# A windowed-attention and sticky-router kernel: the TensorE work of each attention step put in the order of its tile shapes, and two PSUM rings exchanged

## The chip, the core and the metric

The kernel runs on one core of a Trainium2 chip. The metric is the device time of one execution in microseconds (us). The kernel before was timed in three runs; their median is 696.66 us. The engines are TensorE (PE in the profile, with its weight loads as PEld), VectorE (DVE), ScalarE (ACT), GpSimd (POOL) and SyncE (SP), which issues most transfers. The program keeps eight PSUM tiles of 128 x 512 fp32 values, ps0 to ps7, one bank each; TensorE writes its results there, and VectorE and ScalarE read them.

## The reference, cut to what matters

Eight batches of eight heads are attended to. Each head has 512 local tokens, which see the local tokens at most 32 positions away and all 32 global tokens, and 32 global tokens that see all. The 576 rows of 512 values that come out per batch go through a router (eight experts, with a gate that may keep the expert of the row before) and then through the chosen expert, two layers of 512 x 1024.

```python
s_ll = np.where(abs(pos_q - pos_k) <= 32, scale * q_l @ k_l.T, -1e9)
a_l = softmax(concat([scale * q_l @ k_g.T, s_ll]))        # local rows
out_l = a_l @ concat([v_g, v_l])
out_g = softmax(scale * q_g @ concat([k_g, k_l]).T) @ concat([v_g, v_l])
x = concat([out_g, out_l])                                # 576 x 512 per batch
logits = x @ w_gate; local_gate = sigmoid(x @ w_local)
e = argmax(logits) if s == 0 or local_gate < 0.5 else the expert of the row before
out = softmax(logits)[e] * (relu(x @ w1[e]) @ w2[e])
```

## The kernel before, in words

The program has an attention part, the first 240 us or so, a routing part that is worked in between, and the experts' products, which fill the rest. The change is in the attention part alone (class Attn).

**Units and steps.** The work of a batch is cut into six units: four local ones, l0 to l3, each a pair of heads, and two global ones, g0 and g1, each two pairs. They run in the order l0, l1, g0, l2, g1, l3 (the list `order` in `run`), 48 units in all. One pass of the loop in `run` is called a step here. A step computes the scores of one unit (`nx`) and finishes the unit of two steps earlier (`st`). The six steps of a batch are numbered by the unit whose scores they compute:

| step | scores of | finishes |
|---|---|---|
| 0 | l0 | g1 of the batch before |
| 1 | l1 | l3 of the batch before |
| 2 | g0 | l0 |
| 3 | l2 | l1 |
| 4 | g1 | g0 |
| 5 | l3 | l2 |

**What a step issues.** The instructions of each engine stand in the order in which the code records them (the schedule is manual). For a local unit, in two halves hb of 256 rows each:

- `l_s` (L238, L243): a product with an identity puts the mask into a PSUM bank (L238, a tile of 128 x 128), and eight products per half add the scores (L243, stationary tiles of 128 rows by 64 columns). The two products of a pair fill different column halves.
- `l_max` (L248, L250, on VectorE): the row maximum, and the scores minus the maximum, written to SBUF. This frees the bank. `l_exp` (L254) is the exponential on ScalarE.
- `l_t` (L260, L262): two steps later, eight 128 x 128 transposes, and two copies on ScalarE out of PSUM.
- `l_av` (L276): the products with v, stationary tiles of 128 rows by 32 columns, 16 per half, into one bank; then on VectorE the row sums plus 1e-9 (L279), their reciprocals (L281), and the scaled output into the tile xa (L284). L284 frees the bank.

A global unit does the same with `g_s` (L296, 64 columns), `g_max` (L304, L306), `g_exp`, `g_t` (L328, six transposes) and `g_av` (L339, 32 columns).

**The router's pieces.** When a unit of a batch is finished, a piece of x = xa is transposed: `f1` (L352, four transposes of 128 x 128, one for each local unit, copied by ScalarE at L353) and `f1g` (L359, one transpose for the global rows). After the fourth come the router products `f2` (L367) and `f2g` (L375), with 32 columns, then `f3`: four transposes of the logits (L385), a small product (L388), and three VectorE instructions (L390 to L392). They stand in one list, `fin`, from which `fpiece` takes one piece at two places of a step: behind the first scores of the step, and ahead of the v products of the second half.

**Routing in between.** `drip` (called in `l_max`, `g_max`, `l_av`, `g_av`) records one of the routing's small VectorE instructions at a time (`keys`, `probs`, from batch 4 on also `stage_a`, the ranking of tokens by expert).

**PSUM.** The eight banks make three rings, taken in turn: `ps_s`, ps0 to ps3, for scores (and for f3's transposes); `ps_t`, ps4 and ps5, for the transposes l_t, g_t, f1 and f1g; `ps_o`, ps6 and ps7, for l_av, g_av, f2, f2g and f3's small product. Whoever takes a bank waits until its last user has been read out.

A word on tile shapes: 128, 64 and 32 below are the columns of the stationary tile, as the profile's rows have them (128*128, 128*64, 128*32).

## Time and profile before

| what | value |
|---|---|
| median of the three runs (lowest, highest) | 696.66 us (694.63, 696.86) |
| the profiled execution | 694.06 us |
| its span, first to last instruction | 692.3 us |
| PE busy / PEld / DVE / ACT / POOL, share of the span | 97% / 81% / 62% / 50% / 30% |
| DMA | 151.44 MB, mean 219 GB/s |
| TensorE clock granted over the span | 0.995 |

The span is the time from the first to the last instruction of the profiled execution; 1.8 us of its time lie around it. Busy shares are of the whole span. The rows of a timeline give a start, a length from the first start to the last end, the engine, the line and operation, the output and the inputs, the tile (rows*columns of the stationary operand), the number of records, and in brackets the idle time before. A matmul's end is modelled, and matmuls overlap in the rows, so lengths of PE rows overlap too: what a row costs is read here from its start to the start of the next row. An fp32 product appears as two records. A few matmul records are missing.

### The profile page before, as it was taken

How to read it: one execution, taken by the hardware profiler on the slowest of the kernel's cores; microseconds unless marked ns; L12 is line 12 of the kernel's file. 1: busy time of each engine (PE TensorE's matmuls, PEld its weight loads, DVE VectorE, ACT ScalarE, POOL GpSimd, SP SyncE). 2: the span in 40 equal slices, each digit the busy share in tenths (PEclk: the TensorE clock that was granted, in tenths of full speed). 3: DMA queues.
4: the chain of work that ended last, by engine and by line, in shares of the span. 5: the costliest groups of instructions: out<-in, count | busy, mean ns of one | idle time of the engine just before them, and what ended most of it. 6: DMA issues, size and time to landing. Idle time of an engine off the chain costs nothing.

```text
span 692.3 us, 18408 instructions
## 1 busy us (share of the span) xinstructions
PE 670.5 (97%) x7253; PEld 561.1 (81%) x7253; DVE 426.2 (62%) x1050; ACT 342.9 (50%) x614; POOL 207.7 (30%) x342
## 2 busy tenths in 40 slices
PE   9999999999989899998998999999999999999995
PEld 7777777777767787897887988889898889888994
DVE  7878677688887777995517535335354516255572
ACT  4555556555455674653326625344444325255553
POOL 7634334343674301033013303040404020133023
PEclk9999999999999999999999999999999999999999
DMA  8956957866856497777418647337475417265673
GB/s 318 405 220 233 346 193 309 310 248 231 299 196 273 147 356 243 260 243 245 174 60 308 232 149 239 102 117 235 145 225 191 140 61 231 66 222 193 212 270 103
DMA packets 43011, 151.44 MB, mean 219 GB/s; under 512 B 7965, under 2 KB 9245, under 8 KB 38688
## 3 DMA queue, kind: packets, MB, share of 16 engines
q1 hardware_dynamic: 35536, 126.92, 51.6%
q0 software_dynamic: 6960, 21.90, 9.5%
q8 instruction: 77, 1.26, 0.7%
q14 instruction: 150, 1.23, 0.6%
q10 hardware_dynamic: 288, 0.13, 0.1%
HBM read 130.55 MB, written 19.69 MB: 217 GB/s over the span
## 4 chain that ended last, share of the span: by engine, by line
PE 60%; DVE 3%; issue 1%; ACT 0%; POOL 0%; POOLq 0%; DVEq 0%; ACTq 0%
PE ps L1267 29%; PE ps L1256 27%; PE ps L1210 3%; DVE wq L1165 1%; DVE wp L1165 1%; PE ps L1004 0%; PE ps L1379 0%; DVE xl L1165 0%; DVE xT L994 0%; POOL xa L1196 0%; DVE xT L996 0%; POOLq L1427 0%; DVE wp L1213 0%; PE ps L276 0%; DVE wq L1371 0%
## 5 line engine op out<-in xcount | busy, mean ns | idle before, releaser
L1273 POOL DMA_INDIRECT out_dram<-y,tk x39 | 40.4, 1036 | 317.6 <-ACT y L1272 246.3
L1267 PE MATMUL ps<-wp,wq 128*128 128x512 f32 x504 | 128.4, 402 | 1.0 <-ACT wq L1370 1.0
L1267 PEld LDWEIGHTS ps<-wp,wq 128*128 128x128 f32 x504 | 93.5, 190 | 21.1 <-ACT wq L1370 1.2
L1256 PE MATMUL ps<-wp,wp 128*128 128x256 f32 (+5 forms) x672 | 109.3, 322 | 0.2 <-issue 0.2
L1256 PEld LDWEIGHTS ps<-wp,wp 128*128 128x128 f32 x672 | 103.6, 188 | 5.3 <-issue 0.4
L1259 DVE SCALAR_TENSOR_TENSOR wq<-ps,wq 128x256 fp32r<-128x256 f32 (+5 forms) x80 | 41.7, 525 | 72.8 <-ACT wq L1258 62.6
L1213 DVE TENSOR_TENSOR wp<-ps,wp 128x512 fp32r<-128x512 f32 x40 | 27.5, 691 | 78.9 <-ACT wp L1212 78.8
L1258 ACT ACTIVATE wq<-ps 128x256 fp32r<-128x256 f32 (+5 forms) x80 | 37.3, 468 | 78.3 <-PE ps L1256 68.8
L191 POOL TENSOR_SCALAR_AFFINE_SELECT qbd<-raw 64x512 f32<-64x512 f32 x62 | 44.4, 716 | 103.3 <-PE ps L243 85.5
L243 PE MATMUL ps<-kx,qbd 128*64 128x128 f32 x1024 | 71.3, 280 | 0.2 <-issue 0.2
L1272 ACT ACTIVATE y<-ps,pp 128x512 f32<-128x512 f32 x39 | 26.9, 690 | 77.7 <-PE ps L1267 71.1
L243 PEld LDWEIGHTS ps<-kx,qbd 128*64 128x64 f32 x1024 | 55.1, 137 | 12.2 <-issue 7.8
L248 DVE TENSOR_REDUCE mx<-ps 128x4 f32<-128x512 f32 x64 | 43.9, 687 | 29.9 <-PE ps L243 29.9
L1165 DVE TENSOR_TENSOR wp<-raw,wp 128x1024 fp32r<-128x1024 f32 x47 | 57.0, 1217 | 2.8 <-ACT wp L1155 2.8
L254 ACT ACTIVATE pe<-pe 128x512 f32<-128x512 f32 x64 | 40.7, 637 | 31.7 <-DVE pe L250 31.7
L1196 POOL DMA_INDIRECT xa<-xs,idx x42 | 50.9, 1212 | 17.1 <-issue 9.4
L1155 ACT CAST wp<-raw 128x1024 fp32r<-128x1024 f32 x49 | 50.8, 1047 | 0.8 <-ACT hh L1258 0.5
L1212 ACT CAST wp<-ps 128x512 fp32r<-128x512 f32 x40 | 23.4, 590 | 53.9 <-PE ps L1210 53.3
L250 DVE TENSOR_TENSOR pe<-ps,mx 128x512 f32<-128x512 f32 x64 | 44.0, 688 | 1.6
L276 PEld LDWEIGHTS ps<-v,pt 128*32 128x32 f32 x2048 | 33.4, 110 | 13.1 <-issue 7.3
L276 PE MATMUL ps<-v,pt 128*32 128x65 f32 x2048 | 42.8, 222 | 1.1 <-issue 0.4
L262 ACT COPY pt<-ps 128x512 f32<-128x512 f32 x64 | 34.9, 610 | 17.6 <-PE ps L260 17.6
(280 smaller groups left out, 1183.3 us busy)
## 6 DMA issues: line engine op xcount, KB each, us to landing
raw<-in_w_dram SPq DMA_DIRECT2D x78, 512.0 KB, 4.1
v<-in_vw_dram SPq DMA_DIRECT2D x32, 1040.0 KB, 9.8
raw<-in_qk_dram SPq DMA_DIRECT2D x32, 528.0 KB, 8.2
xa<-in_w_dram SPq DMA_DIRECT2D x26, 512.0 KB, 5.2
xT<-in_w_dram SPq DMA_DIRECT2D x20, 512.0 KB, 3.5
xs<-xa SPq DMA_DIRECT2D x8, 1056.0 KB, 4.9
qgb<-in_qg_dram SPq DMA_DIRECT2D x8, 128.0 KB, 3.5
xa<-xs,idx POOLq DMA_INDIRECT x42
```

What stands on the lines that cost most here:

```text
L191: self.nc.gpsimd.affine_select(out=out, in_=in_, pattern=pat, compare_op=ALU.is_ge, fill=0.0, base=0, channel_multiplier=0)
L243: nc.tensor.matmul(sp[64 * t2:64 * t2 + 64, t], qbd[:, w], kf[:, f:f + P], start=False, stop=True, skip_group_check=True)
L248: nc.vector.tensor_reduce(out=mx, in_=st["sp"], axis=AX.X, op=ALU.max)
L250: nc.vector.tensor_tensor(out=st["pe"][:, 4 * hb:4 * hb + 4], in0=st["sp"], in1=mx.broadcast_to([P, 4, P]), op=ALU.subtract)
L254: self.nc.scalar.activation(out=pe, in_=pe, func=AF.Exp, scale=SCALE)
L276: nc.tensor.matmul(o[32 * w4:32 * w4 + 32, g, h], pt[:, 2 * g + w4 // 2, w4 % 2, h, :], v[:, w, h * (D + 1):(h + 1) * (D + 1)], start=True ...
L1155: nc.scalar.copy(out=hi, in_=raw)
L1165: (nc.gpsimd if pool else nc.vector).tensor_tensor(out=lo, in0=raw, in1=hi.bitcast(F32), op=ALU.subtract)
L1196: self.nc.gpsimd.indirect_dma_start(out=self.xr[j] if k == "early" else self.xr4[:, j], out_offset=None, in_=src, in_offset=bass.IndirectO ...
L1256: nc.tensor.matmul(ph, a[:, dc, fs], b_[:, dc, n0:n1], start=(n == 0), stop=(n == 11))
L1259: nc.vector.scalar_tensor_tensor(out=hl[:, fc, n0:n1], in0=ph, scalar=0.0, in1=hh[:, fc, n0:n1].bitcast(F32), op0=ALU.max, op1=ALU.subtract)
L1267: nc.tensor.matmul(py, a[:, fc, js], b_[:, fs], start=(fc == 0 and k == 0), stop=(fc == 7 and k == 2))
```

## The change

Within a step, the instructions of TensorE are put in the order of their tile shapes: first all that uses 128 columns (the transposes l_t or g_t, the masks of both halves, which a new function `l_m` issues ahead of the scores, and the pieces f1, f1g and the transposes of f3, now a function `f3t` of their own), then the scores of both halves (64 columns), then all that uses 32 columns (f2, f2g, f3's small product and the v products of both halves). The one list of pieces becomes two, `wide` for those of 128 columns and `thin` for those of 32, each piece with the step from which it may run; up to two of each are taken in a step. The pieces f1 of l0, l1 and l2 run two steps after their unit was finished, f1 of l3 one step after, f1g two steps after, f2 one and f3 two steps after l3 was finished. And f1 and f1g take their banks from `ps_o` (ps6, ps7) instead of `ps_t`, while f2, f2g and f3's small product take theirs from `ps_t` (ps4, ps5) instead of `ps_o`.

With the order on TensorE the order on VectorE changes too: L248 and L250 of both halves (L252 and L254 in the changed code) come ahead of the three instructions of each half's v products.

```diff
+    def l_m(self, st):
+        nc = self.nc
+        b, pr = st["u"]
+        if pr == 0:
+            self.cur[b]["xa"] = self.xa()
+            self.cur[b]["xg"] = self.xg()
+        st["pe"] = self.pe()
+        st["sps"] = [self.bank(self.ps_s) for _ in range(2)]
+        for hb, sp in enumerate(st["sps"]):
+            mo = sp.rearrange("p t (k c) -> p t k c", c=32)[:, :, 0::3, :]
+            nc.tensor.matmul(mo, self.cst.idb, self.mask[:, 4 * hb:4 * hb + 4], start=True, stop=False, skip_group_check=True)
+
     def l_s(self, st, hb):
         nc = self.nc
-        if hb == 0:
-            b, pr = st["u"]
-            if pr == 0:
-                self.cur[b]["xa"] = self.xa()
-                self.cur[b]["xg"] = self.xg()
-            st["pe"] = self.pe()
         qbd = st["qbd"]
         kf = st["kx"].rearrange("p m c k -> p (m c k)")
-        sp = st["sp"] = self.bank(self.ps_s)
-        mo = sp.rearrange("p t (k c) -> p t k c", c=32)[:, :, 0::3, :]
-        nc.tensor.matmul(mo, self.cst.idb, self.mask[:, 4 * hb:4 * hb + 4], start=True, stop=False, skip_group_check=True)
+        sp = st["sps"][hb]
...
-        tp = self.bank(self.ps_t)
+        tp = self.bank(self.ps_o)
...
     def f2(self, b):
         nc = self.nc
-        gp = self.ps_o()
+        gp = self.ps_t()
...
+    def f3t(self, b, queue=True):
+        lp = self.cur[b]["lp"] = self.bank(self.ps_s if queue else self.ps_t)
+        for tg in range(4):
+            self.nc.tensor.transpose(lp[:, tg], self.gsb[:, P * tg:P * tg + P], self.cst.idf)
+
     def f3(self, b, rt, queue=True):
         nc = self.nc
         c = self.cur[b]
         b4 = b % 4
-        lp = self.bank(self.ps_s if queue else self.ps_t)
-        for tg in range(4):
-            nc.tensor.transpose(lp[:, tg], self.gsb[:, P * tg:P * tg + P], self.cst.idf)
-        gp3 = self.ps_o()
+        lp = c["lp"]
+        gp3 = self.ps_t()
...
-        fin = []
-        when = []
-
-        def fpiece():
-            if fin and when[0] <= s:
-                f, a = fin.pop(0)
-                when.pop(0)
-                if f is not None:
-                    f(*a)
+        wide, thin = [], []
+
+        def fpiece(q, m=1):
+            while m and q and q[0][0] <= s:
+                _, f, a = q.pop(0)
+                f(*a)
+                m -= 1
...
             if nl:
+                self.l_m(nx)
+            fpiece(wide, 2)
+            if nl:
                 self.l_s(nx, 0)
                 self.l_max(nx, 0)
+                self.l_s(nx, 1)
+                self.l_max(nx, 1)
             else:
                 self.g_s(nx)
                 self.g_max(nx)
-            fpiece()
+            fpiece(thin, 2)
+            if nl:
+                self.l_exp(nx, 0)
+            else:
+                self.g_exp(nx)
             if sl:
                 self.l_av(st, 0)
-            if nl:
-                self.l_exp(nx, 0)
-                self.l_s(nx, 1)
-                self.l_max(nx, 1)
-            fpiece()
-            if not nl:
-                self.g_exp(nx)
-            if sl:
                 self.l_av(st, 1)
             if sg:
                 self.g_av(st)
             if st is not None:
                 b, i = st["u"]
                 if sl:
-                    fin.append((self.f1, (b, i)))
+                    wide.append((s + 1 + (i < 3), self.f1, (b, i)))
                     if i == 3:
-                        fin += [(self.f2, (b,)), (self.f3, (b, rt))]
+                        thin.append((s + 1, self.f2, (b,)))
+                        wide.append((s + 2, self.f3t, (b,)))
+                        thin.append((s + 2, self.f3, (b, rt)))
                 elif i == 1:
-                    fin += [(self.f1g, (b,)), (None, ()), (self.f2g, (b,))]
-            if len(fin) > 4:
-                fpiece()
-            when += [s + 1] * (len(fin) - len(when))
+                    wide.append((s + 2, self.f1g, (b,)))
+                    thin.append((s + 2, self.f2g, (b,)))
...
...
+        self.f3t(b, False)
         self.f3(b, rt, False)
```

The places at which the prediction looks, as the program's order has them; ps, xa, pt and the like are tiles with their numbers, and x4 is the count of instructions in a row.

TensorE before, step 1 of a batch in the steady part, from its first mask to the first instructions of step 2:

```order
L238 LDWEIGHTS idb_82
L238 MATMUL ps3_66<-mask_154,idb_82 128x4x2x32
L243 MATMUL ps3_66<-kx1_147,qbd1_145 64x128 x8
L359 MATMUL ps4_67<-idf_81,xg1_111 128x128
L276 MATMUL ps6_69<-v2_134,pt2_142 32x65 x16
L238 LDWEIGHTS idb_82
L238 MATMUL ps0_63<-mask_154,idb_82 128x4x2x32
L243 MATMUL ps0_63<-kx1_147,qbd1_145 64x128 x8
L276 MATMUL ps7_70<-v2_134,pt3_143 32x65 x16
L260 MATMUL ps5_68<-idf_81,pe2_139 128x128 x4
L260 MATMUL ps4_67<-idf_81,pe2_139 128x128 x4
L296 MATMUL ps1_64<-raw0_77,qgb0_152 64x256
```

In the changed kernel, TensorE in the same step, from its first mask:

```order
L236 MATMUL ps3_66<-mask_154,idb_82 128x4x2x32
L236 LDWEIGHTS idb_82
L236 MATMUL ps0_63<-mask_154,idb_82 128x4x2x32
L356 MATMUL ps6_69<-idf_81,xa1_109 128x128 x4
L247 MATMUL ps3_66<-kx1_147,qbd1_145 64x128 x8
L247 MATMUL ps0_63<-kx1_147,qbd1_145 64x128 x8
L280 MATMUL ps7_70<-v2_134,pt2_142 32x65 x16
L280 MATMUL ps6_69<-v2_134,pt3_143 32x65 x16
L264 MATMUL ps5_68<-idf_81,pe2_139 128x128 x4
L264 MATMUL ps4_67<-idf_81,pe2_139 128x128 x4
L363 MATMUL ps7_70<-idf_81,xg1_111 128x128
L356 MATMUL ps6_69<-idf_81,xa1_109 128x128 x4
```

Both masks now stand ahead, the piece f1 (L356) follows them into ps6, the scores of both halves stand together, and f1g (L363) and f1 of l3 (L356) come right behind step 2's transposes, into ps7 and ps6, the two banks that the v products (L280) of step 1 have just filled.

TensorE before, from the last scores of step 3 into step 4:

```order
L243 MATMUL ps0_63<-kx0_146,qbd0_144 64x128 x8
L385 MATMUL ps1_64<-idf_81,gsb_113 128x128 x4
L388 MATMUL ps7_70<-sel_85,gsb21_115 32x9
L276 MATMUL ps6_69<-v4_136,pt3_143 32x65 x16
L328 MATMUL ps4_67<-idf_81,pg0_148 128x128 x3
L328 MATMUL ps5_68<-idf_81,pg0_148 128x128 x3
L296 MATMUL ps2_65<-raw2_79,qgb0_152 64x256
L296 MATMUL ps2_65<-raw3_80,qgb0_152 64x256
L296 MATMUL ps3_66<-raw2_79,qgb0_152 64x288
L296 MATMUL ps3_66<-raw3_80,qgb0_152 64x288
L352 MATMUL ps4_67<-idf_81,xa0_108 128x128 x4
L352 MATMUL ps5_68<-idf_81,xa0_108 128x128 x4
```

In the changed kernel, TensorE in the same place:

```order
L247 MATMUL ps0_63<-kx0_146,qbd0_144 64x128 x8
L395 MATMUL ps5_68<-sel_85,gsb21_115 32x9
L280 MATMUL ps7_70<-v4_136,pt2_142 32x65 x16
L280 MATMUL ps6_69<-v4_136,pt3_143 32x65 x16
L332 MATMUL ps4_67<-idf_81,pg0_148 128x128 x3
L332 MATMUL ps5_68<-idf_81,pg0_148 128x128 x3
L356 MATMUL ps7_70<-idf_81,xa0_108 128x128 x4
L300 MATMUL ps2_65<-raw2_79,qgb0_152 64x256
L300 MATMUL ps2_65<-raw3_80,qgb0_152 64x256
L300 MATMUL ps3_66<-raw2_79,qgb0_152 64x288
L300 MATMUL ps3_66<-raw3_80,qgb0_152 64x288
```

The piece f1 of l0 (L356) has moved ahead of the global scores, and from ps4 to ps7, the bank of the first v products (L280) of step 3.

VectorE before, step 1, from the first maximum to the end of the second half's output:

```order
L248 TENSOR_REDUCE mx0_118<-ps2_65 128x4
L771 MEMSET xa1_109 128x4x7
L250 TENSOR_TENSOR pe0_137<-ps2_65,mx0_118 128x512
L279 TENSOR_SCALAR rs2_123<-ps7_70 128x4
L774 COPY gx_276<-tok_256 32x1
L281 RECIPROCAL rs2_123<-rs2_123 128x4
L284 TENSOR_TENSOR xa0_108<-ps7_70,rs2_123 128x2x128
L248 TENSOR_REDUCE mx1_119<-ps3_66 128x4
L250 TENSOR_TENSOR pe0_137<-ps3_66,mx1_119 128x512
L279 TENSOR_SCALAR rs0_121<-ps6_69 128x4
L281 RECIPROCAL rs0_121<-rs0_121 128x4
L284 TENSOR_TENSOR xa0_108<-ps6_69,rs0_121 128x2x128
```

VectorE in the changed kernel, the same step:

```order
L252 TENSOR_REDUCE mx0_118<-ps2_65 128x4
L254 TENSOR_TENSOR pe0_137<-ps2_65,mx0_118 128x512
L252 TENSOR_REDUCE mx1_119<-ps3_66 128x4
L254 TENSOR_TENSOR pe0_137<-ps3_66,mx1_119 128x512
L283 TENSOR_SCALAR rs2_123<-ps6_69 128x4
L285 RECIPROCAL rs2_123<-rs2_123 128x4
L288 TENSOR_TENSOR xa0_108<-ps6_69,rs2_123 128x2x128
L283 TENSOR_SCALAR rs0_121<-ps7_70 128x4
L285 RECIPROCAL rs0_121<-rs0_121 128x4
L288 TENSOR_TENSOR xa0_108<-ps7_70,rs0_121 128x2x128
```

The output of the first half (L288 from ps6) now stands behind the maximum and the subtraction of the second half (L252, L254).

More of the change, by code (lines that the diff above doesn't have):

```diff
@@ L247, in l_max @@
         mx = self.mx()
-        nc.vector.tensor_reduce(out=mx, in_=st["sp"], axis=AX.X, op=ALU.max)
+        nc.vector.tensor_reduce(out=mx, in_=st["sps"][hb], axis=AX.X, op=ALU.max)
         self.drip()
-        nc.vector.tensor_tensor(out=st["pe"][:, 4 * hb:4 * hb + 4], in0=st["sp"], in1=mx.broadcast_to([P, 4, P]), op=ALU.subtract)
+        nc.vector.tensor_tensor(out=st["pe"][:, 4 * hb:4 * hb + 4], in0=st["sps"][hb], in1=mx.broadcast_to([P, 4, P]), op=ALU.subtract)
     def l_exp(self, st, hb):
@@ L357, in f1g @@
         c = self.cur[b]
-        tp = self.bank(self.ps_t)
+        tp = self.bank(self.ps_o)
         nc.tensor.transpose(tp[:, 0], c["xg"].rearrange("p a d -> p (a d)"), self.cst.idf)
@@ L372, in f2g @@
         c = self.cur[b]
-        gp2 = self.ps_o()
+        gp2 = self.ps_t()
         for h in range(4):
@@ L511, in run @@
                 if sl:
-                    fin.append((self.f1, (b, i)))
+                    wide.append((s + 1 + (i < 3), self.f1, (b, i)))
                     if i == 3:
-                        fin += [(self.f2, (b,)), (self.f3, (b, rt))]
+                        thin.append((s + 1, self.f2, (b,)))
+                        wide.append((s + 2, self.f3t, (b,)))
+                        thin.append((s + 2, self.f3, (b, rt)))
                 elif i == 1:
-                    fin += [(self.f1g, (b,)), (None, ()), (self.f2g, (b,))]
-            if len(fin) > 4:
-                fpiece()
-            when += [s + 1] * (len(fin) - len(when))
+                    wide.append((s + 2, self.f1g, (b,)))
+                    thin.append((s + 2, self.f2g, (b,)))
         self.drip(1000)
-        moe.tail = self.tail(units[n - 2], units[n - 1], fin, rt, moe)
+        moe.tail = self.tail(units[n - 2], units[n - 1], [x[1:] for x in wide], rt, moe)
+        assert not thin
     def tail(self, sg, sl, fin, rt, moe):
         b = B - 1
-        fin = [x for x in fin if x[0] is not None]
         self.g_t(sg)
```

## The prediction

> **What bounds the kernel now.** I read the page first, then two stages of the attention part. In a stage's row stand its stretch, its length, and the busy time of PE, PEld, DVE, ACT and POOL.
>
> ```profile
> PE 670.5 (97%) x7253; PEld 561.1 (81%) x7253; DVE 426.2 (62%) x1050; ACT 342.9 (50%) x614; POOL 207.7 (30%) x342
> ```
>
> ```profile
> 37.48:149.15 111.67, 111.26 (x2356) 84.82 (x2349) 84.68 (x291) 64.06 (x148) 44.24 (x97) 1.00 0.74 272
> 149.15:211.34 62.19, 59.41 (x1229) 44.87 (x1222) 50.56 (x182) 32.11 (x74) 35.10 (x70) 1.00 0.70 255
> ```
>
> The first stage holds four whole batches, from one step 2 to another: 27.92 us each, with TensorE busy for 111.26 of 111.67 us. VectorE is busy for 84.68 us, 21.2 per batch, or 76%. The second holds two batches in which the ranking of tokens is worked in: 62.19 us, 6.3 more than two plain ones. So TensorE's stream is the bound, and VectorE is second. The list of waits over 20 to 230 us says the same (engine, output and line, what it waited for: us in total, times, longest):
>
> ```profile
> POOL qbd L191 <- PE ps L243: 85.5, 21, 6.5
> DVE mx L248 <- PE ps L243: 28.8, 37, 1.4
> ACT pt L262 <- PE ps L260: 17.6, 14, 2.5
> PEld ps L352 <- DVE xa L284: 2.4, 6, 0.8
> PE ps L352 <- DVE xa L284: 1.0, 2, 0.6
> ```
>
> Everyone waits for TensorE; it waits little itself, but where it does, it is the x transposes (L352) that wait for VectorE's output of the v products (L284). Then the stream itself, step 1 of a batch with what stands around it. What a row costs is the distance of its start to the next row's.
>
> ```profile
> 84.26 0.88 PE L328 MATMUL ps<-idf,pg 128*128 128x128 f32 x6
> 84.97 0.27 PE L238 MATMUL ps<-mask,idb 128*128 128x256 bf16 x1
> ...
> 87.92 0.89 PE L339 MATMUL ps<-v,ptg 128*32 128x65 f32 x48
> 88.74 1.09 PE L260 MATMUL ps<-idf,pe 128*128 128x128 f32 x8
> 89.67 0.27 PE L238 MATMUL ps<-mask,idb 128*128 128x256 bf16 x1
> 89.87 1.09 PE L243 MATMUL ps<-kx,qbd 128*64 128x128 f32 x16
> 90.89 0.33 PE L359 MATMUL ps<-idf,xg 128*128 128x128 f32 x1
> 91.15 0.67 PE L276 MATMUL ps<-v,pt 128*32 128x65 f32 x32
> 91.75 0.28 PE L238 MATMUL ps<-mask,idb 128*128 128x256 bf16 x1
> 91.96 1.09 PE L243 MATMUL ps<-kx,qbd 128*64 128x128 f32 x16
> 92.98 0.67 PE L276 MATMUL ps<-v,pt 128*32 128x65 f32 x32
> 93.58 1.09 PE L260 MATMUL ps<-idf,pe 128*128 128x128 f32 x8
> 94.61 1.14 PE L296 MATMUL ps<-raw,qgb 128*64 128x256 f32 x8
> ```
>
> **Term one: the changes of shape that go.** Six transposes take 0.71 us (84.26 to 84.97) and eight 0.93 (88.74 to 89.67), both followed by a mask of the same shape: 0.11 each, and 0.05 too much at the group's start. The same eight followed by another shape take 1.03 (93.58 to 94.61): 0.10 more at the end. So a change of shape costs 0.15 us. The v products agree: 48 records take 0.82, 32 take 0.60, so 16 take 0.22 and 0.16 is left over. The weight loads show where it goes, with the idle time in brackets:
>
> ```profile
> 88.73 0.86 PEld L260 LDWEIGHTS ps<-idf,pe 128*128 128x128 f32 x8
> 89.56 0.10 PEld L238 LDWEIGHTS <-idb 128*128 128x128 bf16 x1
> 89.87 0.85 PEld L243 LDWEIGHTS ps<-kx,qbd 128*64 128x64 f32 x16 [0.21 <-issue]
> ```
>
> Within a shape a load runs beside the matmuls before it; at the change to 64 columns the first load waits 0.21 us for nothing but the issue. The Trainium skill (TensorE: Matmul & The Clock Gate, Part 2) says that the queue pulls weight loads ahead of running matmuls where the row groups don't conflict or the background weights are the target; by that a change of shape would be free, which these rows contradict, and the sum below would lack this term.
>
> In the program's order a batch changes shape 34 times before and 18 times after (three per step). Over the attention part, up to the last scores, it is 271 and 149: 122 fewer, 18.3 us at 0.15. Bounds: 0.10 (the end alone), 12 us; 0.17 (a mask between two other shapes takes 0.20, and I allow for a cheaper one), 21 us. I take 0.15, since two kinds of rows give it. No operation is added; every product and transpose still runs.
>
> **Term two: the waits that come.** TensorE takes its instructions in order, so one that waits holds all behind it. Two do, each time the x transposes. VectorE's rows:
>
> ```profile
> 91.01 0.69 DVE L248 TENSOR_REDUCE mx<-ps 128x4 f32<-128x512 f32 x1 [0.79 <-PE ps L243]
> ...
> 93.25 0.68 DVE L248 TENSOR_REDUCE mx<-ps 128x4 f32<-128x512 f32 x1
> 93.97 0.69 DVE L250 TENSOR_TENSOR pe<-ps,mx 128x512 f32<-128x512 f32 x1
> 94.58 0.15 DVE L279 TENSOR_SCALAR rs<-ps 128x4 f32<-128x4 f32 x1
> 94.76 0.18 DVE L281 RECIPROCAL rs<-rs 128x4 f32<-128x4 f32 x1
> 94.97 0.42 DVE L284 TENSOR_TENSOR xa<-ps,rs 128x256 f32<-128x256 f32 x1
> 95.33 0.94 DVE L304 TENSOR_REDUCE m<-ps 128x1 f32<-128x256 f32 x2
> ...
> 103.90 0.30 DVE L391 TENSOR_REDUCE L<-ps 128x36 f32<-128x144 f32 x1
> 103.92 0.07 DVE L390 MEMSET L<- 128x9 f32 x1
> 104.23 0.17 DVE L392 COPY L<-ps 32x9 f32<-32x9 f32 x1
> 104.42 0.16 DVE L279 TENSOR_SCALAR rs<-ps 128x4 f32<-128x4 f32 x1
> ```
>
> The first maximum starts 1.14 us after the first score product (89.87 to 91.01); I count from there, where VectorE is told. A half's maximum and subtraction take 0.72 + 0.61 = 1.33 (93.25, 93.97, 94.58). Output of a half of v products: 0.18 + 0.21 to the start of L284, whose record is 0.42 long, and the next instruction starts 0.36 after it: 0.75 in all.
>
> *Step 1 into step 2.* In the new order VectorE does both halves of scores first: 2.66. The first output starts there, ends at 2.66 + 0.39 + 0.42 = 3.47; the second ends at 4.22. TensorE meanwhile: the two blocks of scores take 1.02 + 0.87 (the second without a change), the v products 0.60 + 0.44, so its step ends 2.93 after the first score product, 1.79 after the count's start. Then come step 2's transposes, 0.93, and f1g, 0.11. At 2.83 stands f1 of l3. It reads the xa that the second output writes, and takes that output's bank. It waits for 4.22: 1.4 us. Behind it stand the global scores, f2, and the v products of step 2; VectorE, out of work, waits for those. Before, this piece ran between the v products of step 2, when the output was long done.
>
> *Step 3 into step 4.* Here f3's three instructions (103.90 to 104.42, 0.52) stand ahead of the outputs: the first ends at 3.99. TensorE's next step begins with six transposes: 1.79 + 0.71 = 2.50. Then f1 of l0 wants a bank of `ps_o`, and the next in turn is that of step 3's first v products. It waits 1.5 us (in batch 0, which has no f3 yet, 1.0). Its data were ready a step ago; before, it stood behind the global scores and took a bank of `ps_t`. The global scores, g0's v products and the whole of step 5 are queued behind it.
>
> What the other steps need is ready: masks take banks that were read a step before; f1 of l1 and l2 find banks freed by ScalarE's copy or an older output; `f3t`'s bank was read by g0's exponentials; kx and qbd are made by POOL, which waits 85.5 us for TensorE. The transfers keep their order on SP. VectorE's small routing instructions go between dependent ones. None of that gets later than by the waits themselves.
>
> Bounds: VectorE may start late by work left over from the step before (steps 5 and 1 hold 4.2 us of it each, and step 0 between them two halves of scores, 2.7, and more): up to 0.6 more per wait. It may be 0.3 less, if two instructions pack closer than in these rows. 7 batches have the first wait (the last batch's f1 of l3 lies in the tail), 8 the second: 7 x 1.4 + 7 x 1.5 + 1.0 = 21.3 us, from 17 to 30.
>
> **Term three: the ranking.** In 149 to 211 us VectorE has 50.56 - 2 x 21.2 = 8.2 us more to do. Before, most of it cost TensorE's stream something already (6.3 us more). After, about half of it falls where TensorE waits for VectorE, 4 us, and I take half of that as new: 2 us, from 0 to 4.
>
> **Sum.** -18.3 + 21.3 + 2.0 = +5.0 us. On the profiled execution that is 694.06 + 5.0 = 699.1 us. That execution lies 2.6 below the median of the runs, so the median to expect is 696.66 + 5.0 = 701.7 us. A measurement of this kernel tells some 0.3%, 2.1 us, from no change. What follows the attention part (the tail, the experts) is only shifted: its pieces keep their order but for two banks.
>
> **The rivals.**
>
> *The terms cancel.* With 0.17 per change, or waits of 1.2 us, the sum is within 2.1 us of nothing: 697. The sum is a difference of two terms of 20, so this is near. 0.17.
>
> *Only the wait for data holds.* If the bank at step 4 is free when f1 of l0 comes, its 11.5 us go: 696.7 - 18.3 + 9.8 + 2.0 = 690.2. For it: VectorE is idle for 24% of a batch. Against: the order of its instructions, above; the bank would have to be free 1.5 us sooner. 0.08.
>
> *Faster by the whole of term one.* If the outputs are through within 2.83 us of the first score signal instead of 4.22, no new wait arises: 678.4. For it speaks only that nearly nobody is waited for now; against it that four instructions of 0.61 to 0.72 stand ahead of the outputs. 0.07.
>
> *VectorE becomes the bound.* Its 21.2 us per batch would have to follow without a gap from step 5 to step 1, with the routing's instructions no longer between dependent ones, and each wait grows by 0.6: 15 x 0.6 = 9 more, and the ranking's upper end 2 more: 712. The Trainium skill (TensorEngine Tiling, PSUM Bottleneck) warns that faster matmuls do not make the reading of PSUM faster, and that it may become the bottleneck; the waits of VectorE for TensorE, 28.8 us, say that it isn't yet. 0.13.
>
> *A change of shape is free after all* (the loads' idle time would be hidden by the matmuls): no first term, 696.7 + 23.3 = 720. The two kinds of rows speak against it. 0.03.
>
> **How the numbers follow.** The forecast has 0.52, with its own range from 697 to 709. Faster: 0.08 + 0.07 = 0.15. Same: 0.17. Slower: 0.52 + 0.13 + 0.03 = 0.68. The range from 690 to 710 leaves out the whole saving, the free change, and part of VectorE as the bound: under 0.2.
>
> **What would show it right or wrong.** Right: in the plain batches each step of the changed kernel has three changes of shape; two idle times of PE per batch, ahead of L356, ended by VectorE's L288, near 1.4 and 1.5 us; a batch of about 28.4 us (27.92 - 16 x 0.15 + 2.9); VectorE's maximum, subtraction, maximum, subtraction without a gap. Wrong: L356 without idle time, and a batch near 25.5 us; or idle time ahead of the masks, the scores or the v products; or an idle time at L356 ended by ScalarE; or an equal number of idle weight loads.

## The result, and the profile after

The changed kernel takes 706.32 us, median of four runs (704.65 to 707.47), the kernel before 696.44 on the same chip (694.63 to 696.86): 1.0145 times as long, with a 95% interval of 1.0118 to 1.0172, or 9.9 us more. The forecast was 5.0 more. The profiled execution after took 707.47 us with a span of 705.7. On another chip the pair came out at 701.19 and 692.60 us, 1.0138 (1.0114 to 1.0161). The kernel before differs by up to 0.7% between the chips used (691.58 to 696.44 us), so times are compared below as ratios to the kernel before on the same chip, and stretches by their microseconds in the traces.

The busy row of the page after, and the two stages that were read before, each from a step 2 to a step 2 (stretch, its length, then the busy time of PE, PEld, DVE, ACT, POOL):

```profile
PE 662.4 (94%) x7253; PEld 564.5 (80%) x7253; DVE 424.2 (60%) x1050; ACT 342.8 (49%) x614; POOL 209.1 (30%) x342
```

```profile
36.70:152.54 115.84, 105.84 (x2355) 85.20 (x2349) 85.52 (x293) 64.34 (x149) 44.23 (x97) 1.00 0.72 265
152.54:217.71 65.17, 56.88 (x1208) 45.60 (x1202) 48.36 (x174) 31.45 (x74) 33.54 (x68) 0.97 0.64 234
```

In the four plain batches TensorE is busy for 105.84 us where it was busy for 111.26, so the fewer changes of shape did bring something. But the stage has become 4.17 us longer: TensorE is now idle for 10.0 us of it, before for 0.4. The waits of 20 to 240 us say for whom it waits:

```profile
DVE mx L252 <- PE ps L247: 28.7, 20, 2.3
...
PE ps L356 <- DVE xa L288: 7.0, 15, 1.0
PE ps L363 <- DVE xa L288: 5.9, 7, 1.6
...
PE ps L332 <- DVE L L399: 4.3, 6, 0.8
```

Before, the x transposes waited for 1.0 us in all. Now they wait for 7.0 (f1) and 5.9 (f1g), and the global transposes for another 4.3. TensorE's stream around the places that the forecast named, step 2 (from 94.47) and step 4 (from 105.37):

```profile
94.47 1.09 PE L264 MATMUL ps<-idf,pe 128*128 128x128 f32 x8
96.33 0.33 PE L363 MATMUL ps<-idf,xg 128*128 128x128 f32 x1 [0.76 <-DVE xa L288]
97.07 0.66 PE L356 MATMUL ps<-idf,xa 128*128 128x128 f32 x4 [0.41 <-DVE xa L288]
97.66 1.14 PE L300 MATMUL ps<-raw,qgb 128*64 128x256 f32 x8
...
105.37 0.55 PE L332 MATMUL ps<-idf,pg 128*128 128x128 f32 x3
106.74 0.55 PE L332 MATMUL ps<-idf,pg 128*128 128x128 f32 x3 [0.82 <-DVE L L399]
107.75 0.66 PE L356 MATMUL ps<-idf,xa 128*128 128x128 f32 x4 [0.46 <-DVE xa L288]
108.33 1.14 PE L300 MATMUL ps<-raw,qgb 128*64 128x256 f32 x8
```

In step 2, f1 of l3 starts 2.60 us after the step's head; with eight transposes (0.93) and f1g (0.11) ahead of it, it would start after 1.04. That is a wait of 1.56, forecast 1.4. It comes in two parts, since f1g already has to wait for a bank. In step 4, f1 of l0 starts 2.38 us after the head instead of 0.71: a wait of 1.67, forecast 1.5. But its first part lies at a place that the forecast had not named: the second half of the global transposes (L332) waits for a bank of `ps_t`, which f3's small product holds until VectorE has copied it (L399). And VectorE, ahead of step 2:

```profile
92.80 0.68 DVE L252 TENSOR_REDUCE mx<-ps 128x4 f32<-128x512 f32 x1
93.52 0.69 DVE L254 TENSOR_TENSOR pe<-ps,mx 128x512 f32<-128x512 f32 x1
94.13 0.68 DVE L252 TENSOR_REDUCE mx<-ps 128x4 f32<-128x512 f32 x1
94.84 0.69 DVE L254 TENSOR_TENSOR pe<-ps,mx 128x512 f32<-128x512 f32 x1
...
95.85 0.42 DVE L288 TENSOR_TENSOR xa<-ps,rs 128x256 f32<-128x256 f32 x1
...
96.59 0.43 DVE L288 TENSOR_TENSOR xa<-ps,rs 128x256 f32<-128x256 f32 x1
```

Maximum, subtraction, maximum, subtraction follow without a gap, and the outputs only then, as forecast: f1g starts 0.06 us after the end of the first output, f1 0.05 after the end of the second.

### The profile page after: what moved, and what is told of

Read it like the earlier page. It is cut to its first block, busy times and chain, and to the rows that moved or that the text cites. A ratio compares the mean times of both kernels' runs of the same rounds, so it can differ in the third digit from the quotient of the medians.

```text
span 705.7 us, 18429 instructions
## 1 busy us (share of the span) xinstructions
PE 662.4 (94%) x7253; PEld 564.5 (80%) x7253; DVE 424.2 (60%) x1050; ACT 342.8 (49%) x614; POOL 209.1 (30%) x342
## 4 chain that ended last, share of the span: by engine, by line
PE 56%; DVE 6%; issue 1%; ACT 1%; POOL 0%; POOLq 0%; DVEq 0%; ACTq 0%
PE ps L1274 27%; PE ps L1263 25%; PE ps L1217 2%; DVE wp L1172 1%; DVE wq L1172 1%; DVE hl L1266 1%; PE ps L1386 0%; DVE xT L1001 0%; DVE xl L1172 0%; DVE xT L1003 0%; POOL xa L1203 0%; DVE o L917 0%; PE ps L1011 0%; POOLq L1434 0%; DVE wp L1220 0%
## 5 line engine op out<-in xcount | busy, mean ns | idle before, releaser
L247 PE MATMUL ps<-kx,qbd 128*64 128x128 f32 x1024 | 66.6, 283 | 1.3 <-issue 0.9
L247 PEld LDWEIGHTS ps<-kx,qbd 128*64 128x64 f32 x1024 | 57.4, 141 | 8.2 <-issue 4.6
L252 DVE TENSOR_REDUCE mx<-ps 128x4 f32<-128x512 f32 x64 | 43.8, 684 | 30.4 <-PE ps L247 29.6
L254 DVE TENSOR_TENSOR pe<-ps,mx 128x512 f32<-128x512 f32 x64 | 44.0, 688 | 1.4
L191 POOL TENSOR_SCALAR_AFFINE_SELECT kx<-raw 128x384 f32<-128x384 f32 (+3 forms) x127 | 42.7, 369 | 3.2 <-DMA raw<-in_qk_dram 1.1
L280 PEld LDWEIGHTS ps<-v,pt 128*32 128x32 f32 x2048 | 32.3, 110 | 10.2 <-issue 8.4
L280 PE MATMUL ps<-v,pt 128*32 128x65 f32 x2048 | 37.4, 221 | 1.9 <-issue 1.8
```

Source lines behind the costliest of these rows:

```text
L191: self.nc.gpsimd.affine_select(out=out, in_=in_, pattern=pat, compare_op=ALU.is_ge, fill=0.0, base=0, channel_multiplier=0)
L247: nc.tensor.matmul(sp[64 * t2:64 * t2 + 64, t], qbd[:, w], kf[:, f:f + P], start=False, stop=True, skip_group_check=True)
L252: nc.vector.tensor_reduce(out=mx, in_=st["sps"][hb], axis=AX.X, op=ALU.max)
L254: nc.vector.tensor_tensor(out=st["pe"][:, 4 * hb:4 * hb + 4], in0=st["sps"][hb], in1=mx.broadcast_to([P, 4, P]), op=ALU.subtract)
L280: nc.tensor.matmul(o[32 * w4:32 * w4 + 32, g, h], pt[:, 2 * g + w4 // 2, w4 % 2, h, :], v[:, w, h * (D + 1):(h + 1) * (D + 1)], start=True ...
```

## The experiments

Theory W is that of the forecast: the fewer changes of shape save time on TensorE, and a few waits behind VectorE's later outputs cost more than that. Rival V: VectorE as a whole can't keep the pace, whatever its order. Rival R: the exchange of the rings is the cause. The table holds every kernel. "Batch" is the mean over the four plain batches, from step 2 of the second batch to step 2 of the sixth; "late" is the stretch from there to the transposes that open the tail, 2 2/3 batches with the ranking of tokens in them. Both are distances between starts of transposes in each kernel's timeline of TensorE.

| kernel | batch, us | late, us | ratio to before (95% interval) | median, us | before there |
|---|---|---|---|---|---|
| before | 27.92 | 84.59 | 1 | 696.44 | 696.44 |
| changed | 28.96 | 92.34 | 1.0145 (1.0118 to 1.0172) | 706.32 | 696.44 |
| after_again | 28.83 | 90.64 | 1.0138 (1.0114 to 1.0161) | 701.19 | 692.60 |
| e1 outputs first | 27.65 | 93.60 | 1.0127 (1.0103 to 1.0152) | 700.63 | 691.75 |
| e2 f1 of l0 later | 28.57 | 90.51 | 1.0090 (1.0067 to 1.0112) | 698.59 | 691.75 |
| e3 wide behind global | 28.37 | 92.88 | 1.0142 (1.0115 to 1.0169) | 702.30 | 691.75 |
| e4 rings back | 31.87 | 102.50 | 1.0480 (1.0454 to 1.0505) | 725.77 | 691.75 |
| e5 before, maxima first | 30.18 | 93.91 | 1.0335 (1.0274 to 1.0395) | 713.07 | 692.60 |
| e6 before, masks together | 27.44 | 84.50 | 0.9981 (0.9964 to 0.9997) | 691.27 | 692.60 |
| e8 x all later | 31.63 | 92.08 | 1.0326 (1.0305 to 1.0346) | 714.34 | 692.60 |
| e9 no-wait order | 28.75 | 94.45 | 1.0194 (1.0169 to 1.0220) | 704.92 | 692.13 |
| e10 e2 and f3's bank | 28.17 | 91.63 | 1.0101 (1.0071 to 1.0131) | 699.29 | 692.13 |
| e11 outputs first, early batches | 27.42 | 91.46 | 1.0105 (1.0079 to 1.0130) | 699.07 | 692.13 |
| e12 mended e9 | 26.80 | 84.66 | 0.9898 (0.9880 to 0.9917) | 684.90 | 691.58 |

**after_again: the changed kernel unedited.**

> The changed kernel once more, unedited, beside the kernels of this call. Every theory: 1.012 to 1.017 times the kernel before. It tells one thing: whether the idle time of 1.95 us that its first profiled execution has between the v products of the last batch's step 2, ended by nothing but the issue, comes again (then it belongs to the change), or not (then it belongs to that execution).

It does not come again: the first execution had three idle times of 0.41 to 0.46 us among the v products of the last batch's step 2, the second had none. So some 2 us of the first execution's late stage belong to that execution. What ended those idle times stays open. Its two stages:

```profile
36.05:151.36 115.31, 105.93 (x2350) 85.22 (x2348) 85.11 (x291) 64.07 (x148) 43.81 (x97) 1.00 0.73 266
151.36:217.12 65.76, 57.94 (x1208) 46.63 (x1201) 48.33 (x174) 31.67 (x75) 33.31 (x68) 0.95 0.64 237
```

**e1: VectorE does the outputs ahead of the second half's maximum.** `self.l_max(nx, 1)` moves behind the v products; TensorE's order stays.

```diff
                 self.l_s(nx, 1)
-                self.l_max(nx, 1)
...
             if sg:
                 self.g_av(st)
             if nl:
+                self.l_max(nx, 1)
                 if s in DEFER:
```

> Only VectorE's order changes: in a local step the second half's maximum and subtraction go behind the two outputs of the v products; TensorE's stream is that of the changed kernel. Theory W (the two waits of the x transposes eat what the fewer changes of shape bring): the outputs are through about 1.5 us sooner, both waits nearly vanish, 706.3 less 16 to 22 us of waits: 682 to 690 us, faster than both kernels. Rival V (VectorE has too much to do from step 5 to step 1, its order does not matter): the wait only moves to the second half of the weights, 702 to 707 us. Rival R (the exchange of the rings is what costs): 704 to 708 us.

1.0127: hardly less than the changed kernel, so as a forecast for the whole it missed. By the table it splits: a batch has become 1.2 us shorter (28.83 to 27.65), and the late stage 3.0 longer (90.64 to 93.60). On the scale of the first chip 1.0127 is 705.3 us, where V and R had it; but the shorter batch shows that order matters, which speaks against V. `l_max` also issues the routing's small instructions (`drip`), so moving it moved these, and in the late stage that shows. On SP the load of the next pair stands behind a batch's stores, and POOL waits 11.91 us for it:

```profile
162.92 0.38 SPq L420 DMA_DIRECT2D xs<-xa  x1
...
167.22 0.36 SPq L178 DMA_DIRECT2D raw<-in_qk_dram  x1
```

```profile
170.82 1.49 POOL L191 TENSOR_SCALAR_AFFINE_SELECT qbd<-raw 64x512 f32<-64x512 f32 x2 [11.91 <-DMA raw<-in_qk_dram]
...
186.76 10.51 POOL L914 TENSOR_SCALAR o<-io,plo 128x128 bf16<-128x128 bf16 x18 [8.17 <-DVE rs L285]
```

TensorE does not wait for POOL at that place. Its two longest waits in this stage are for a scan of the ranking on VectorE (2.06 us, at the global transposes) and for POOL's keys at the scores (2.54 us, at 199.14), behind the 10.51 us in which POOL makes the ranking's tables (L914). In the two profiles of the changed kernel the first does not occur, and the longest for POOL's keys is 0.47 us. Whether the late load is what brought these waits about isn't shown.

**e11: the same, but only until the ranking begins** (from step 30 on the changed kernel's order).

> Outputs ahead of the second half's maximum, but only up to the step at which the ranking of tokens begins; from there on the order of the changed kernel. If the gain of the first experiment in the plain batches (1.6 us each) was given back by the ranking's own order (a load queued on SP behind the ranking's stores, a scan on VectorE ahead of a bank): the first five batches keep 5 to 8 us, and the ranking's batches take what they take in the changed kernel, so 694 to 697 us on the chip where the changed kernel takes 701. Rival (the gain is lost again in any case, since the end is set by POOL or the transfers): 700 to 702.

The split holds: four batches take 109.66 us instead of 115.31, 1.4 us less each, and the late stage is that of the changed kernel (91.46 and 90.64). The median, 699.07, misses the forecast by 2 us: of its four runs the profiled one took 695.97, the others 698.93 to 699.22, so the traced gain is that of the best execution. No wait of TensorE for VectorE is listed in these four batches, and a batch of 27.42 us is shorter than in the kernel before (27.92). So the order on VectorE costs the changed kernel 1.2 (e1) to 1.4 us a plain batch, and e1's small result is a gain that the ranking's batches took back.

**e2: f1 of l0 one step later; e3: f1g and f1 of l3 behind the global scores.**

```diff
-                    wide.append((s + 1 + (i < 3), self.f1, (b, i)))
+                    wide.append((s + 1 + (i < 3) + (i == 0), self.f1, (b, i)))
```

```diff
-            fpiece(wide, 2)
+            if nl or nx["u"][1] == 1:
+                fpiece(wide, 2)
...
                 self.g_max(nx)
+                if nx["u"][1] == 0:
+                    fpiece(wide, 2)
```

> The x transposes f1 of l0 come one step later, in step 5 with f1 of l1, rather than at the head of step 4; nothing else. Theory W: the wait for a bank in step 4, 1.5 us as forecast and 1.67 as the trace has it, goes in 8 batches, and a little comes back in step 5 where four more transposes stand: 12 us less at most, 694 to 699 us. Rival V (VectorE's work is the bound, the wait shows wherever TensorE first needs VectorE): 704 to 708 us. Rival that the bank does not matter but only the data of f1 of l3: 704 to 708 as well.

> Where the next scores are those of g0 (step 2), the x transposes stand behind the global scores instead of ahead of them; the place of f1 of l0 in step 4 stays. Theory W: the wait for the data of f1 of l3, 1.4 us as forecast and 1.56 as the trace has it, loses the 1.06 us that the global scores take, and one change of shape comes back (0.15) and some of the copy behind it is seen by f2: 0.5 to 0.9 less in 7 batches, 700 to 703 us. Rival V: 705 to 708 us.

Each takes a part of one wait away: in the third batch step 4 goes from 4.85 to 3.72 us in e2, while step 5 grows by 0.45; in e3 step 2 goes from 6.09 to 5.69. For the whole e2 gains about half a per cent (1.0138 to 1.0090), e3 nothing that can be told (1.0142). The forecasts start from the 706.3 us of the first chip; by their ratios e2 would take 702.7 there and e3 706.3. So W's ranges are missed, though the 698.59 and 702.30 of this faster chip fall into them. e3's plain batches are shorter by 0.46 us, its late stage is 2.2 longer. e2 shows why it is less than forecast: of step 4's wait 0.82 us isn't that of f1.

```profile
104.42 0.55 PE L332 MATMUL ps<-idf,pg 128*128 128x128 f32 x3 [0.82 <-DVE L L399]
```

**e10: e2, and f3's small product in a bank of the scores' ring.**

```diff
-        gp3 = self.ps_t()
+        gp3 = self.ps_s() if queue else self.ps_t()
```

> The kernel with f1 of l0 one step later, and besides f3's small product in a bank of the scores' ring rather than of the ring that the transposes of step 4 want next. One edit on that kernel. If the wait of 0.82 us in step 4 (second half of the global transposes, ended by VectorE's copy of f3's product) hangs on that bank alone: step 4 takes 2.9 to 3.2 us instead of 3.73, 7 batches, 4 to 6 us less than that kernel: 692 to 695 us where it took 698.6. Rival (whatever stands there next waits for VectorE just as long): no change.

The wait of L332 goes, but the v products of the same step then wait 0.52 us for a bank of `ps_o`, and the whole takes what e2 took (1.0101, 1.0090). The rival was nearer: there is a queue of users behind one late reader. (The row names L283; VectorE does it right behind the output of the first half, which ends at 106.08.)

```profile
106.23 0.89 PE L343 MATMUL ps<-v,ptg 128*32 128x65 f32 x48 [0.52 <-DVE rs L283]
```

**e4: the rings exchanged back.** f1 and f1g take `ps_t` again, f2, f2g and f3's product `ps_o`; the order is that of the changed kernel.

> The exchange of the two rings of PSUM banks is undone, the order stays: f1 and f1g take their banks from the ring of the pe transposes again, f2, f2g and the routing's product from that of the v products. Theory W: the wait of f1 of l3 for its data stays (1.5 us a batch), f1 of l0 no longer waits for VectorE's output but for a bank that ScalarE must copy out, and the routing's product waits for a bank of the v products: 698 to 710 us, and no gain of more than 8. Rival R (the exchange of the rings is the whole cause of the loss): under 692 us.

Both missed: 1.0480, 24 us over the changed kernel. TensorE waits for VectorE's copy of f3's product where the second half of the v products wants its bank, and the x transposes wait for ScalarE's copies at L266:

```profile
112.15 0.67 PE L280 MATMUL ps<-v,pt 128*32 128x65 f32 x32 [1.84 <-DVE L L399]
...
119.67 0.66 PE L356 MATMUL ps<-idf,xa 128*128 128x128 f32 x4 [0.45 <-ACT pt L266]
```

R falls with it: given the new order, the exchange saves 3 us a batch.

**e5: the kernel before, with VectorE's new order alone.** `l_av` is cut in two, and the first half's output is recorded behind the second half's maximum; TensorE's order and the rings stay.

```diff
             if sl:
-                self.l_av(st, 0)
+                o = self.l_av(st, 0)
             if nl:
                 self.l_exp(nx, 0)
                 self.l_s(nx, 1)
                 self.l_max(nx, 1)
+            if sl:
+                self.l_out(st, 0, o)
```

> The kernel before, with its TensorE order, and with VectorE doing the second half's maximum and subtraction ahead of the first half's output, as in the changed kernel. Theory W: the order on VectorE costs only where something stands close behind it; here the x transposes stand among the v products, so the time stays within 3 us of the kernel before. Rival (VectorE's order by itself makes the loss): 7 us slower or more.

The forecast missed by far: 1.0335, 20 us, which is the rival's outcome. Here no x transpose stands close behind. In step 3 f3's small product takes the other bank of `ps_o` between the two halves of the v products, so the second half wants the first half's bank back, and VectorE reads that with the output that was put off (L290, to 109.33):

```profile
108.91 0.42 DVE L290 TENSOR_TENSOR xa<-ps,rs 128x256 f32<-128x256 f32 x1
109.27 0.29 DVE L397 TENSOR_REDUCE L<-ps 128x36 f32<-128x144 f32 x1
109.29 0.07 DVE L396 MEMSET L<- 128x9 f32 x1
109.60 0.17 DVE L398 COPY L<-ps 32x9 f32<-32x9 f32 x1
```

```profile
109.39 0.67 PE L276 MATMUL ps<-v,pt 128*32 128x65 f32 x32 [1.58 <-DVE L L396]
```

The row of TensorE names L396, a memset that runs beside; the copy out of f3's bank (L398) starts only after the product, so that bank isn't what it waited for. So W has to be put more widely: with outputs that come 1.3 us later, whoever next wants one of the two banks of that ring waits, not the x transposes as such. In e4 and e5 it is the second half of the v products, in e10 those of a global unit.

**e6: the kernel before with both masks together.** The second half's mask moves up behind the first, by the function `l_m` of the change; nothing else moves.

```diff
             if nl:
+                self.l_m(nx)
                 self.l_s(nx, 0)
```

> The kernel before, with the second half's mask moved up behind the first one, next to the transposes; nothing else moves. It takes one change of shape out of each local step that has v products, 30 in all, and leaves every other order as it was. A change at 0.15 us: 4.5 us faster (3.0 by the lower price of 0.10, 5.1 by 0.17). Rival (a change of shape is free): the same time within 1 us. Rival (what a mask saves is given back, since VectorE becomes the bound): the same time, with TensorE waiting for VectorE.

0.9981 (0.9964 to 0.9997): 1.3 us faster, not 4.5. TensorE's rows show the price (the mask that stood ahead of 91.09 is gone):

```profile
88.90 0.38 PE L236 MATMUL ps<-mask,idb 128*128 128x256 bf16 x2
89.21 1.09 PE L247 MATMUL ps<-kx,qbd 128*64 128x128 f32 x16
...
90.49 0.67 PE L280 MATMUL ps<-v,pt 128*32 128x65 f32 x32
91.09 1.09 PE L247 MATMUL ps<-kx,qbd 128*64 128x128 f32 x16
92.11 0.67 PE L280 MATMUL ps<-v,pt 128*32 128x65 f32 x32
```

This step 1 takes 4.74 us, before 4.84; steps 3 and 5 lose 0.10 or 0.11 each as well. In step 0 the mask stood behind f1, which has its shape, so no change goes there: it is three changes a batch and not four, and the expectation's 30 counts such steps. So a change costs 0.10 to 0.11 us. The mean batch is 0.48 us shorter, but the second plain batch before holds a stop of 0.41 us on the issue (84.05); the other three are 0.27 to 0.42 shorter. In the late stage nothing is left of it (84.50 and 84.59). The 1.3 us of the whole (0.2 to 2.5 by the interval) would not by themselves rule out the rival of a free change; the rows do.

**e8: all that hangs on the two waits one step on.** f1 of l0 in step 5, f1 of l3, f2 and f2g in step 3, f3 in step 4.

> The changed kernel with what hangs on the two waits moved one step on: f1 of l0 to step 5, f1 of l3 and both router products to step 3, f3 with its transposes to step 4. The number of changes of shape and VectorE's order stay. Theory W: neither wait remains, a batch takes 25.5 to 26.3 us, 8 batches gain 2.5 to 3.2 us each on the changed kernel: 18 to 25 us less than it, 8 to 15 less than the kernel before. Rival V (VectorE cannot follow at that pace): a wait for VectorE or ScalarE comes up elsewhere, and the batch stays at 27.5 us or more, within 3 us of the kernel before or slower.

1.0326, with a batch of 31.63 us: by its numbers V's outcome. But the cause isn't VectorE's pace. f3 starts the routing of a batch, and with it the store of its rows. One step later, VectorE has to wait with the outputs of the next batch but one, and TensorE waits for VectorE:

```profile
110.80 0.42 DVE L288 TENSOR_TENSOR xa<-ps,rs 128x256 f32<-128x256 f32 x1 [5.64 <-DMA xs<-xa]
```

```profile
111.28 0.98 PE L343 MATMUL ps<-v,ptg 128*32 128x65 f32 x28 [3.81 <-DVE xa L288]
```

In e8 and e9 a batch's store is recorded after the first writes into its buffer for the batch after next, so part of the rows stored are of another batch; the amount of work is the same.

**e9: an order meant to have no waits.** f1g in step 1, f1 of l0 in step 5, f1 of l3 at the end of step 2 in a bank of `ps_s`, f2 in step 3, f3 at the end of step 3 with its small product in a bank of `ps_s`.

> A version built so that nothing of the routing stands where VectorE is late: f1g one step earlier (step 1), f1 of l0 one step later (step 5), f1 of l3 at the end of step 2 behind the v products and in a bank of the scores' ring, f2 at step 3, f3's small product and its transposes at the end of step 3, the small product in a bank of the scores' ring too. Changes of shape: about 19 per batch as in the changed kernel, VectorE's order in a step as there. Theory W (the loss sits in the few waits for banks and data behind the late outputs): no wait left of over 0.3 us, a plain batch of 25.6 to 26.5 us, the whole 8 to 16 us below the kernel before. Rival V (VectorE and ScalarE can't keep the pace): a batch stays above 27.3, the whole within 4 us of the kernel before or above it.

1.0194, with a batch of 28.75 us, above V's limit, and again it is the store. In the order of recording four small routing instructions now come after the v products of step 3 rather than with them. The store goes at 97.28, in step 3, where in the changed kernel (after_again) it goes at 91.32, in step 1, and an output waits for it. The rows are of e9's SP, after_again's SP, and e9's VectorE:

```profile
97.28 0.38 SPq L422 DMA_DIRECT2D xs<-xa  x1
```

```profile
91.32 0.38 SPq L420 DMA_DIRECT2D xs<-xa  x1
```

```profile
101.81 0.42 DVE L288 TENSOR_TENSOR xa<-ps,rs 128x256 f32<-128x256 f32 x1 [4.28 <-DMA xs<-xa]
```

**e12: e9 mended.** Four routing instructions are issued right behind f3, and f1g and f1 of l1 go to the ends of steps 2 and 5, next to transposes, in banks of `ps_s`.

```diff
+            fpiece(last, 2)
...
-                    wide.append((s + 1 + (i < 3), self.f1, (b, i)))
-                    if i == 3:
-                        thin.append((s + 1, self.f2, (b,)))
-                        wide.append((s + 2, self.f3t, (b,)))
-                        thin.append((s + 2, self.f3, (b, rt)))
+                    if i == 1:
+                        last.append((s + 2, self.f1, (b, 1, self.ps_s)))
+                    elif i < 3:
+                        wide.append((s + 2 + (i == 0), self.f1, (b, i)))
+                    else:
+                        last.append((s + 1, self.f1, (b, 3, self.ps_s)))
+                        thin.append((s + 2, self.f2, (b,)))
+                        last.append((s + 2, self.f3, (b, rt)))
                 elif i == 1:
-                    wide.append((s + 2, self.f1g, (b,)))
-                    thin.append((s + 2, self.f2g, (b,)))
+                    last.append((s + 2, self.f1g, (b, self.ps_s)))
+                    thin.append((s + 3, self.f2g, (b,)))
```

> The rearranged version with two faults mended: the routing's own small instructions keep the pace of the changed kernel (four of them are issued right behind f3, so that the store of a batch's rows leaves before the buffer is written again), f1g stands at the end of step 2 and f1 of l1 at the end of step 5, both in banks of the scores' ring. Changes of shape and VectorE's order in a step as in the changed kernel; the orders on SP and POOL are those of the changed kernel. Theory W: no wait of TensorE of over 0.3 us in a plain batch, a batch of 25.6 to 26.4 us (before 27.9, changed kernel 28.7), the ranking's batches about as much better: 8 to 16 us below the kernel before. Rival V (VectorE and ScalarE can't keep the pace): a batch stays above 27.3, and the whole within 4 us of the kernel before.

684.90 us against 691.58: 0.9898 (0.9880 to 0.9917), 6.7 us faster than the kernel before and, by the ratios, some 17 faster than the changed kernel. The four plain batches as one stretch, and one batch from step 2:

```profile
35.85:143.06 107.21, 103.96 (x2350) 85.87 (x2348) 83.74 (x291) 63.52 (x148) 43.60 (x96) 1.00 0.79 289
```

```profile
62.58 1.09 PE L264 MATMUL ps<-idf,pe 128*128 128x128 f32 x8
63.60 1.14 PE L300 MATMUL ps<-raw,qgb 128*64 128x256 f32 x8
64.67 1.13 PE L280 MATMUL ps<-v,pt 128*32 128x65 f32 x64
65.73 0.33 PE L363 MATMUL ps<-idf,xg 128*128 128x128 f32 x1
65.90 0.60 PE L356 MATMUL ps<-idf,xa 128*128 128x128 f32 x4
66.34 1.04 PE L264 MATMUL ps<-idf,pe 128*128 128x128 f32 x8
...
88.43 1.09 PE L264 MATMUL ps<-idf,pe 128*128 128x128 f32 x8
```

The batch from 62.58 to 88.43 takes 25.85 us, with the changed kernel's number of changes of shape per batch (18) and VectorE's new order. No wait for VectorE's outputs is left in these rows; the longest for VectorE that its list of waits has in the four batches is 0.2 us. That settles W against V: VectorE, with the same work, keeps this pace. The numbers of the forecast were missed all the same: 6.7 us lies under 8 to 16, and the mean batch of 26.80 above 25.6 to 26.4. The four batches hold 2.7 us of stops that nothing but the issue ends (see the last section), and the late stage took 84.66 us, what it takes in the kernel before.

## Why the prediction was right, and where it was off

The direction, the mechanism and the range held; the size was half. Point by point:

- **Stream and waits.** As forecast, TensorE's busy time fell, and waits behind VectorE's outputs came at steps 2 and 4. By the fastest batch of e12 (25.85), which has as many changes of shape and almost no waits, the changed kernel's batch of 28.74 (after_again, from 93.53) holds 2.89 us of waits. Forecast were 1.4 + 1.5 = 2.9. That the two agree to 0.01 is luck: read from the starts of the rows the waits are 1.56 and 1.67, and by the means of four batches (28.83 and 26.80, with e12's stops in the latter) it is 2.0.
- **Term one was mis-sized.** A change of shape was put at 0.15 us, from the sum of an end effect (0.10) and a start effect (0.05). e6 measures 0.10 to 0.11, the end effect alone, for the one kind of change that it takes out (32, 128, 64 columns become 32, 64). Less directly, 27.79 in the batch before that starts at 93.58, less the 25.85 of e12, for 16 changes, is 0.12, with all that e12 moves besides. With 122 changes the term is 12.8 us at 0.105 and 14.6 at 0.12, rather than 18.3. Then a batch comes to 27.92 - 1.7 + 2.9 = 29.1, or 28.9 at 0.12, and 28.83 and 28.96 were measured; forecast was 28.4. The Trainium skill (TensorE: Matmul & The Clock Gate, Part 2) lets weight loads go ahead of running matmuls; by that, as the prediction reads it, e6 would have brought nothing, and each change that it took out brought 0.10 to 0.11.
- **Term two held in size, not in every place.** The wait of step 4 was put down to a bank of `ps_o` alone. Half of it is the wait of the global transposes for f3's bank in `ps_t`, hence e2 takes 0.7 us off a batch (the third, 28.61 to 27.92) and not 1.5. And in step 2, f1g waits ahead of f1.
- **Term three was too small.** The late stage grew by 6.05 us (after_again). By the plain batches, 2 2/3 x 0.9 = 2.4 of it were to come, so the ranking costs 3.6, forecast 2 (0 to 4, so within the bounds). Most of it is one wait: the first product of the placing of tokens wants a bank of `ps_o` behind a late output. This row is of after_again; the kernel before has no such wait.

```profile
205.90 0.17 PE L968 MATMUL ps<-sumA,on 128*128 128x8 bf16 x1 [2.69 <-DVE xa L288]
```

- **The sum again.** With the forecast's 21.3 for the waits, -14.6 + 21.3 + 3.6 = +10.3 us, or +12.1 with -12.8, against 9.9 and 8.6 measured. The waits of all batches were not measured apart, so the sum fits but proves no single term. What lies ahead of the second batch and behind the attention part differs by 1 to 2 us between executions, with both signs, and isn't explained further.
- **The rivals.** The terms don't cancel: a change costs less than was taken, not more. (At 0.17 a change the prediction's own sum is +2.6 us, not within 2.1 of nothing.) Both waits are there, so neither rival with fewer of them holds. VectorE is not the bound (e11, e12). A change is not free (e6). What the forecast had not weighed at all is that undoing the exchange of rings would cost 24 us (e4), and that VectorE's order costs 20 us in the kernel before without any of the new places on TensorE (e5).

Only half answered is why e12 and e6 gain nothing in the late stage. TensorE's listed waits there add up to 7.7 us in e12 and 4.2 in e6, against 3.4 in the kernel before, so what the order saves goes into waits. In e12 3.7 us of them are for ScalarE's copies of the global weights, 2.38 at one place. What holds these copies up wasn't tried; in the kernel before POOL is busy there for 12.2 us on end with the tables of the ranking.

## What to carry to other kernels

Where instructions of one engine are sorted to save its own overhead, the engines that follow it are sorted with them: work out when the last reader of each bank comes in the new order, and who takes that bank next. In a ring of two banks, as here, a late reader is somebody's wait, and freeing one user may only hand the wait to the next (e10); placing the users so that none comes right behind the late reader does free it (e12). And look at what rides along with a call that is moved: a store that leaves late can hold a buffer two rounds on (e8, e9), and a load can get behind a store (e1, where its price isn't shown).

## What was not expected of the hardware

A change between stationary tiles of 128, 64 and 32 columns costs 0.10 to 0.12 us, though the first weight load behind it is mostly idle for 0.17 to 0.21; where 128 columns follow 32, none is listed (as at 88.73 in the prediction's rows). In the kernel before, behind a mask and behind scores:

```profile
86.89 0.85 PEld L243 LDWEIGHTS ps<-kx,qbd 128*64 128x64 f32 x16 [0.21 <-issue]
87.91 0.73 PEld L339 LDWEIGHTS ps<-v,ptg 128*32 128x32 f32 x48 [0.17 <-issue]
```

TensorE also stops now and then, mostly within a row of v products, ended by nothing but the issue: in e12 five times in the four plain batches, for 0.21 to 0.90 us, in the kernel before once, for 0.4; in the two profiles of the changed kernel two of them come at the same place of the program (48.06 and 46.85, 60.89 and 59.94), the three of the last batch in one alone. What it waits for, the profile doesn't show. The longest, in a step 2 of e12:

```profile
92.20 0.64 PE L280 MATMUL ps<-v,pt 128*32 128x65 f32 x26 [0.90 <-issue]
```
